# Attention heads one after the other, then a mixture of experts: the hash and the product with v start a step later in the first batch, and the sign follows its hash directly in the second

## The chip, the core and the metric

The kernel runs on one core of a Trainium2 chip. Five engines work from queues of their own, each in the order in which the program gives it work: TensorE (PE, with its weight loads as PEld), VectorE (DVE), ScalarE (ACT), GpSimd (POOL) and SyncE (SP), which issues most transfers. An engine that waits for another holds up all that stands behind the waiting instruction in its own queue. The metric is the time on the device in microseconds, as the median of several runs.

## The reference, cut to what matters

Inputs are q, k and v of shape 2 x 8 x 768 x 64 (batch, head, position, channel), a projection of 64 x 6, and the probabilities and weights of four experts.

```python
q_bits = (einsum('bhsd,dk->bhsk', q, proj) > 0)      # six hash bits per position
k_bits = (einsum('bhsd,dk->bhsk', k, proj) > 0)
mask = q_bucket[:, :, :, None] == k_bucket[:, :, None, :]
scores = where(mask, q @ k.T / sqrt(64), -1e9)
attn = softmax(scores)                                # each row
x = (attn @ v), heads side by side                    # 1536 x 512
out = sum over e of p[:, e] * (relu(x @ w1[e]) @ w2[e])
```

Everything is float32. Products that have to be exact are computed from a high and a low part of each number, as three products.

## The kernel before

**Heads and steps.** The sixteen heads (b, h) follow one another; a head has six steps, t0 to t5, one for each 128 rows of q. `attention()` is a generator that goes through the steps; in each it does the operations of `ORDER = "TXSUVMEYNRP"` in that order, and each belongs to the step by a lag:

- S (`stage_s`): four matmuls give the scores of 128 rows (two with q1 and k1, L368, and two with q2 and k2, L370, which add the mask from the hash bits). VectorE then takes the row minimum and copies the scores out of PSUM (L375). This operation is called the minimum below.
- E: ScalarE's exponential of the step before (L391).
- T, for the first nine heads (`mixed`): TensorE transposes the tile of three steps before into two PSUM tiles (L438); ScalarE and VectorE copy them out (L442, L444). In t1 and t4 ScalarE copies both, in the other steps each copies one. For the other seven heads X and Y do this with VectorE and DMA.
- V (`stage_v`): the product with v, in two parts for the first nine heads. With the lags 4 and 6 of `LAG_V` the first part stands in t3 and the second in t5 of the next head. Head (0, 7) has its own lags, 4 and 5.
- U (`stage_u`): ScalarE and VectorE copy the product out (L520, L522), in t2 of the head after that. `u_lag` adds the last lag of V and `LAG_U`: 6 + 3.
- M (`stage_m`): GpSimd divides by the row sums, for two heads at once, so only behind odd heads: the first half in t3, the second in t4 of the head two later. In the first batch each half is three GpSimd instructions (L533, L535, L538). They thus run in heads 3, 5 and 7 of the first batch.
- N: a reciprocal on VectorE (L405), in t2.
- P: the next piece of `prep_head`, the preparation of the next head.

Within one step, M and S come ahead of P.

**The preparation of a head.** `prep_head` is a generator, and each step takes one piece of it. For the heads in `BLOCKS` (2 to 8 and 11 to 15) the pieces are: in t0 VectorE transposes q and k (L293); in t1 they are split into a high part ah (ScalarE, L230) and a low part al (VectorE, L231, which needs ah), and GpSimd makes three copies of ah (L221); in t2 TensorE computes the hash, six matmuls into the PSUM tile hps (L315), and GpSimd copies al into ah; in t3 ScalarE takes the sign (L324), and GpSimd makes the bits from it (L327) and copies twelve rows (L221), after which S of the next head can run its second pair. Heads 9 and 10, (1, 1) and (1, 2), are transposed on TensorE and have one piece less: split in t0, hash in t1, sign and bits in t2. Heads 0 and 1 have code of their own.

**PSUM.** The scores, hps and the PSUM tiles of TensorE's transposes of q and k share two buffers (`big`). V, T and the expert layers share four (`one`).

**Expert weights beside the first batch.** Until the first batch is through, the main loop counts in i how often `attention()` yields; T, S and each piece of P yield once. From i = 42 on, every sixth yield gives one step of the splitting of the first weights: in most of them a cast on VectorE (L665) and a subtraction on GpSimd (L658), eight subtractions in all. A head of six steps with four pieces of P has 16 yields.

**Afterwards.** The heads of the second batch run between the matmuls of the expert layers of the first batch; then the expert layers of the second batch run alone, with fewer products.

Of the kernel before, what the change touches and what calls it, by code (L numbers as in the profile page):

```python
# [10 lines left out]
ACTF = mybir.ActivationFunctionType  # L11
# [7 lines left out]
SGN_SCALE = float(2**20)  # L19
# [4 lines left out]
LAG_T = 3  # L24
LAG_X = 2
LAG_Y = 4
LAG_V = ((4, 6), (7,))
LAST_V = (4, 5)
LAG_U = (3, 1)
LAG_M = (10, 10)  # L30
PP_BUFS = 6
TW = 3
# [17 lines left out]
def tile_lsh_attention__then__domain_moe(  # L50
# [11 lines left out]
    nc = tc.nc  # L62
    B, H, S, D = q.shape
# [12 lines left out]
    NH = S // 2  # L76
# [3 lines left out]
    MKE = MK + 2 * NB  # L80
    scale = 1.0 / float(D) ** 0.5
# [18 lines left out]
    def big(name):  # L100
        return ps2.tile([P, 2, 512], F32, tag="big", name=name)

    def one(name):
        return ps1.tile([P, 512], F32, tag="one", name=name)
# [3 lines left out]
    sgn_bias = const.tile([P, 1], F32, name="sgn_bias")  # L108
# [11 lines left out]
    def two(t):  # L120
        return t.rearrange("p (a n) -> p a n", a=2)
# [65 lines left out]
    def in_blocks(b, h):  # L187
        return b * H + h in BLOCKS
# [27 lines left out]
    def stack_tiles(b, h):  # L216
        heads[b, h] = tuple(stk.tile([P, S], F32R, tag=n, name=n) for n in ("q1", "al", "ah", "k2"))
        return heads[b, h]

    def copy_pool(dst, src):  # L220
        nc.gpsimd.tensor_scalar(out=dst, in0=src, scalar1=1.0, scalar2=1.0, op0=ALU.mult, op1=ALU.mult)  # L221
# [7 lines left out]
    def split_half(dst_hi, dst_lo, src):  # L229
        nc.scalar.activation(dst_hi, src, ACTF.Copy, scale=qk_scale)  # L230
        nc.vector.scalar_tensor_tensor(  # L231
            out=dst_lo, in0=src, scalar=qk_scale, in1=dst_hi.bitcast(F32), op0=ALU.mult, op1=ALU.subtract
        )
# [49 lines left out]
    def prep_head(b, h):  # L283
        second = (b, h) == (0, 1)
        if not second:
            tqk = loaded.pop((0, b, h))
        q1, al, ah, k2 = stack_tiles(b, h)
        if second:
            for ps, sl in zip(in_psum, halves):
                split_half(ah[:, sl], al[:, sl], ps[:, :NH])  # L290
        elif in_blocks(b, h):
            xt = ld.tile([P, S], F32, tag="tqk", name="xt")
            nc.vector.transpose(out=xt, in_=tqk.rearrange("p c r d -> p (c r d)"))  # L293
            yield 0
            split_half(two(ah), two(al), two(xt))
        else:
            ps = big("tps")
            for c in range(NT):
                nc.tensor.transpose(
                    ps[:, c // 3, (c % 3) * P : (c % 3 + 1) * P], tqk[:, c].rearrange("p a d -> p (a d)"), ident  # L300
                )
            split_half(two(ah), two(al), ps[:, :, :NH])
        for rows in (slice(0, D), slice(D, P)):
            copy_pool(q1[rows], ah[0:D].bitcast(F32))
        copy_pool(k2[0:D], ah[D:P].bitcast(F32))
        yield 654
        if second:
            yield 0
            ps = [one("hps1") for _ in range(2)]
        else:  # L310
            hps = big("hps")
            ps = [hps[:, i] for i in range(2)]
        for j, (w, a) in enumerate(((phi, ah), (plo, ah), (phi, al))):
            for i, sl in enumerate(halves):
                nc.tensor.matmul(ps[i][:MKE, :NH], w, a[:, sl], start=j == 0, stop=j == 2)  # L315
        copy_pool(ah[0:D], al[D:P].bitcast(F32))
        if second:
            for i, sl in enumerate(halves):
                nc.scalar.activation(
                    k2[D:MKE, sl], ps[i][D:MKE, :NH], ACTF.Sign, bias=sgn_bias[D:MKE], scale=SGN_SCALE  # L320
                )
        yield 978
        if not second:
            nc.scalar.activation(  # L324
                two(k2[D:MKE]), hps[D:MKE, :, :NH], ACTF.Sign, bias=sgn_bias[D:MKE], scale=SGN_SCALE
            )
        nc.gpsimd.tensor_scalar(  # L327
            out=al[D:MKE],
            in0=k2[D:MKE].bitcast(F32),
            scalar1=1.0,  # L330
            scalar2=bit_mul[D:MKE],
            op0=ALU.add,
            op1=ALU.mult,
        )
        copy_pool(k2[MQ:MQE], al[MK:MKE].bitcast(F32))
        yield 0
# [20 lines left out]
    def mixed(b, h):  # L357
        return b * H + h < LIGHT_FROM
# [189 lines left out]
    def v_lags(b, h):  # L548
        return LAST_V if (b, h) == (0, H - 1) else LAG_V[not mixed(b, h)]

    def u_lag(b, h):
        return v_lags(b, h)[-1] + (1 if (b, h) == (0, H - 1) else LAG_U[not mixed(b, h)])

# [3 lines left out]
    def attention():  # L557
# [3 lines left out]
        def do(op, i):  # L561
# [24 lines left out]
            elif op == "S":  # L586
                if i < n:
                    b, h, t = seq[i]
                    if t == 0:
                        x = hseq.index((b, h))  # L590
                        prep[0] = prep_head(*hseq[x + 1]) if x + 1 < len(hseq) else iter(())
                    stage_s(b, h, t)
                    return 652 + 4270 // NT
# [446 lines left out]
```

## Time and profile before

| | us |
|---|---|
| median of 3 runs | 745.37 (744.41 to 747.24) |
| time of the profiled execution | 746.74 |
| its span, first to last instruction | 744.8 |
| TensorE busy | 721.7 (97% of the span) |
| VectorE busy | 472.6 (63%) |
| ScalarE busy | 298.7 (40%) |
| GpSimd busy | 306.9 (41%) |

Matmuls overlap, so that TensorE's busy time is longer than the time that its array needs. The mean granted clock of TensorE was 0.995 of full speed. The first batch of heads, without expert layers beside it, ends about 146 us from the start of the span; the heads of the second batch end before 460 us.

### The profile page before, as it was taken

The numbers are of one execution on the slowest core, as the hardware profiler recorded it, in microseconds if no ns is written. First come the engines' busy times: TensorE is split into PE (matmuls) and PEld (weight loads), VectorE is DVE, ScalarE is ACT, GpSimd is POOL, SyncE is SP. The second block draws the span as 40 slices with busy tenths as digits, with TensorE's granted clock in tenths as the row PEclk, the third lists the DMA queues.
The fourth block names the chain that finished last, engine by engine and source line by source line (L and its number), as shares of the span: only waits on it lengthen the run. The fifth ranks groups of instructions, "written<-read, shape, count | busy, mean of one in ns | idle before, by whom it ended". The sixth has DMA issues, their size and how long they took to land.

```text
span 744.8 us, 10164 instructions
## 1 busy us (share of the span) xinstructions
PE 721.7 (97%) x3826; PEld 615.3 (83%) x3826; DVE 472.6 (63%) x781; ACT 298.7 (40%) x592; POOL 306.9 (41%) x279
## 2 busy tenths in 40 slices
PE   8988899999989999899999999999999999999998
PEld 6766566697987897879879888998989989899896
DVE  6677676546666666568563323798667686676763
ACT  6777677633232341332422010444334343343430
POOL 5349485423415441445142324754234342343420
PEclk9999999999999999999999999999999999999999
DMA  5224323504686797769767411243021130212302
GB/s 142 44 51 85 72 60 85 85 1 129 162 206 157 213 240 180 193 164 259 217 193 211 115 58 56 67 137 109 30 86 57 63 106 30 85 58 64 105 1 85
DMA packets 85504, 83.05 MB, mean 111 GB/s; under 512 B 49872, under 2 KB 52432, under 8 KB 85456
## 3 DMA queue, kind: packets, MB, share of 16 engines
q1 hardware_dynamic: 84432, 82.08, 40.8%
q8 instruction: 30, 0.49, 0.3%
q10 hardware_dynamic: 1024, 0.33, 0.2%
q14 instruction: 18, 0.15, 0.1%
HBM read 62.68 MB, written 19.71 MB: 111 GB/s over the span
## 4 chain that ended last, share of the span: by engine, by line
PE 87%; ACT 5%; DVE 4%; DMA 2%; issue 1%; POOL 0%; SPq 0%; DVEq 0%; POOLq 0%; ACTq 0%
PE mps L697 12%; PE mps L699 12%; PE mps L698 12%; PE pv L493 9%; PE mps L758 6%; PE mps L757 6%; PE mps L759 6%; PE sps L368 4%; PE sps L370 3%; PE ptps L438 2%; PE mps L912 2%; PE mps L908 2%; PE mps L911 2%; ACT p L391 2%; PE pd L908 2%; PE pa L912 2%
## 5 line engine op out<-in xcount | busy, mean ns | idle before, releaser
L697 PE MATMUL mps<-w2hi,hh 128*128 128x512 f32 (+1 forms) x388 | 150.7, 388 | 0.0
L699 PE MATMUL mps<-w2hi,hl 128*128 128x512 f32 (+1 forms) x388 | 150.5, 388 | 0.0
L698 PE MATMUL mps<-w2lo,hh 128*128 128x512 f32 (+1 forms) x388 | 150.4, 388 | 0.0
L375 DVE TENSOR_SCALAR_CACHE_REDUCE p<-sps 128x768 f32<-128x768 f32 x96 | 90.3, 941 | 32.9 <-PE sps L370 31.2
L391 ACT ACTIVATE p<-p,nb 128x768 f32<-128x768 f32 x96 | 89.5, 932 | 42.3 <-DVE p L375 41.8
L691 DVE SCALAR_TENSOR_TENSOR acc<-mps,pe,acc 128x512 f32<-128x512 f32 (+1 forms) x85 | 63.0, 741 | 63.0 <-PE mps L699 62.6
L763 ACT ACTIVATE hh<-mps 128x384 fp32r<-128x384 f32 x64 | 31.4, 490 | 178.5 <-PE mps L759 178.5
L758 PE MATMUL mps<-xs,w1hi 128*128 128x384 f32 x256 | 87.3, 341 | 0.6 <-POOL xs L538 0.6
L757 PE MATMUL mps<-xs,w1hi 128*128 128x384 f32 x256 | 87.7, 343 | 0.0
L759 PE MATMUL mps<-xs,w1lo 128*128 128x384 f32 x256 | 87.2, 341 | 0.0
L699 PEld LDWEIGHTS mps<-w2hi,hl 128*128 128x128 f32 x388 | 72.8, 188 | 15.6
L894 POOL TENSOR_TENSOR w2lo<-ws,w2hi 128x512 fp32r<-128x512 f32 x32 | 40.5, 1286 | 108.4 <-ACT w2hi L893 108.4
L698 PEld LDWEIGHTS mps<-w2lo,hh 128*128 128x128 f32 x388 | 72.9, 188 | 13.9
L697 PEld LDWEIGHTS mps<-w2hi,hh 128*128 128x128 f32 x388 | 72.8, 188 | 13.8
L764 DVE SCALAR_TENSOR_TENSOR hl<-mps,hh 128x384 fp32r<-128x384 f32 x64 | 35.5, 555 | 73.4 <-ACT hh L763 73.1
L658 POOL TENSOR_TENSOR w1lo<-ws,w1hi 128x512 fp32r<-128x512 f32 x32 | 42.5, 1328 | 79.6 <-DVE w1hi L665 36.1
L658 POOL TENSOR_TENSOR w2lo<-ws,w2hi 128x512 fp32r<-128x512 f32 x32 | 41.2, 1289 | 69.5 <-DVE w2hi L665 55.5
L493 PE MATMUL pv<-pt,tv 128*64 128x384 f32 x288 | 67.3, 492 | 0.0
L221 POOL TENSOR_SCALAR q<-ah 64x768 fp32r<-64x768 f32 (+1 forms) x33 | 32.4, 982 | 72.0 <-ACT ah L230 70.5
L368 PE MATMUL sps<-ah,q 128*128 128x384 f32 x192 | 54.5, 365 | 6.7 <-DVE p L375 3.7
L853 POOL TENSOR_TENSOR w1lo<-ws,w1hi 128x512 fp32r<-128x512 f32 x24 | 37.9, 1588 | 35.6 <-ACT w1hi L849 22.4
L493 PEld LDWEIGHTS pv<-pt,tv 128*64 128x64 f32 x288 | 24.8, 136 | 32.2 <-issue 31.8
(135 smaller groups left out, 1432.8 us busy)
## 6 DMA issues: line engine op xcount, KB each, us to landing
ws<-in_moe_w_dram SPq DMA_DIRECT2D x64, 512.0 KB, 4.0
scr<-t SPq DMA_DIRECT2D x14, 1152.0 KB, 8.7
pt<-scr SPq DMA_DIRECT2D x56, 288.0 KB, 6.1
tv<-in_v_dram SPq DMA_DIRECT2D x16, 192.0 KB, 4.5
out_dram<-acc SPq DMA_DIRECT2D x11, 256.0 KB, 2.0
rdb<-row SPq DMA_DIRECT2D x14, 192.0 KB, 5.2
tqk<-in_q_dram SPq DMA_DIRECT2D x26, 96.0 KB, 3.3
tqk<-in_k_dram SPq DMA_DIRECT2D x24, 96.0 KB, 3.4
```

Of the source, the lines that this page charges most:

```text
L368: nc.tensor.matmul(ps[:, i, :NH], q1[:, sl], k1[:, i * NH : (i + 1) * NH], start=True, stop=False)
L375: nc.vector.tensor_scalar(out=two(pt), in0=ps[:, :, :NH], scalar1=MASKED, scalar2=MASKED, op0=ALU.min, op1=ALU.min, accum_out=nb,)
L391: nc.scalar.activation(pt, pt, ACTF.Exp, bias=nb, scale=-1.0, accum_out=dens[b, h, r][:, o : o + 1])
L493: nc.tensor.matmul(dst, vvs[b, h][:, c], pts[b, h, g][c], start=c == 0, stop=c == NT - 1, tile_position=(0, g * D),)
L658: nc.gpsimd.tensor_tensor(out=lo[:, c - 1], in0=st[c - 1], in1=hi[:, c - 1].bitcast(F32), op=ALU.subtract)
L691: nc.vector.scalar_tensor_tensor(out=acc, in0=ps, scalar=pcol, in1=acc, op0=ALU.mult, op1=ALU.add)
L697: nc.tensor.matmul(ps, hh[:, ts], w2hi[:, f, cs], start=n == 0, stop=False)
L698: nc.tensor.matmul(ps, hh[:, ts], w2lo[:, f, cs], start=False, stop=False)
L699: nc.tensor.matmul(ps, hl[:, ts], w2hi[:, f, cs], start=False, stop=n == FC - 1)
L757: nc.tensor.matmul(ps[:, :SB], w1hi[:, kk, fs], xhi[b, kk][:, sl], start=kk == 0, stop=False)
L758: nc.tensor.matmul(ps[:, :SB], w1hi[:, kk, fs], xlo[b, kk][:, sl], start=False, stop=False)
L759: nc.tensor.matmul(ps[:, :SB], w1lo[:, kk, fs], xhi[b, kk][:, sl], start=False, stop=kk == KD - 1)
```

## The change

Three things change. For heads 2 to 8 (prepared in heads 1 to 7 of the first batch) one empty piece stands ahead of the hash, so that the hash moves from t2 to t3 and the sign with the bits from t3 to t4. For the first nine heads the product with v moves by a step: the first part from t3 to t4, the second from t5 of the next head to t0 of the head after; U stays in t2. For heads 9 to 15 the sign is given right behind the hash, ahead of the next step; the bits stay in t3, and move from t2 to t3 for heads 9 and 10. Heads 2 to 8 have five pieces now, so the head in which they are prepared has 17 yields.

```diff
-LAG_V = ((4, 6), (7,))
+LAG_V = ((5, 7), (7,))
-LAG_U = (3, 1)
+LAG_U = (2, 1)
...
         copy_pool(k2[0:D], ah[D:P].bitcast(F32))
         yield 654
+
+        def sign():
+            nc.scalar.activation(
+                two(k2[D:MKE]), hps[D:MKE, :, :NH], ACTF.Sign, bias=sgn_bias[D:MKE], scale=SGN_SCALE
+            )
+
+        if mixed(b, h) and (second or in_blocks(b, h)):
+            yield 0
         if second:
-            yield 0
             ps = [one("hps1") for _ in range(2)]
         else:
             hps = big("hps")
...
+        if not mixed(b, h):
+            sign()
         yield 978
-        if not second:
-            nc.scalar.activation(
-                two(k2[D:MKE]), hps[D:MKE, :, :NH], ACTF.Sign, bias=sgn_bias[D:MKE], scale=SGN_SCALE
-            )
+        if b and h and not in_blocks(b, h):
+            yield 0
+        if mixed(b, h) and not second:
+            sign()
         nc.gpsimd.tensor_scalar(
             out=al[D:MKE],
```

## Rows read from the trace of the kernel before

**Rows 1.** Windows: length, busy us (count) of PE, PEld, DVE, ACT, POOL; granted clock, DMA.

```profile
22.00:146.00 124.00, 113.00 (x707) 80.00 (x707) 84.14 (x166) 89.85 (x187) 72.40 (x76) 1.00 0.35 72
146.00:460.00 314.00, 308.53 (x1591) 264.48 (x1590) 175.82 (x307) 87.26 (x176) 114.54 (x102) 0.99 0.61 163
```

**Rows 2.** Waits of TensorE from 20 to 140 us: total, times, longest.

```profile
PE hps L315 <- DVE al L231: 4.7, 6, 0.8
PE hps L315 <- ACT ah L230: 4.7, 7, 1.1
```

**Rows 3.** Timeline, TensorE in head 4: start, us, instruction, count, idle time before.

```profile
65.69 0.87 PE L438 MATMUL ptps<-ident,p 128*128 128x128 f32 x6
...
70.56 0.60 PE L315 MATMUL hps<-ah,phi 128*108 128x384 f32 x2 [0.59 <-ACT ah L230]
71.00 0.51 PE L315 MATMUL hps<-ah,plo 128*108 128x384 f32 x2
72.28 0.61 PE L315 MATMUL hps<-al,phi 128*108 128x384 f32 x2 [0.77 <-DVE al L231]
```

**Rows 4.** Chain of waits, the pieces that follow: start, us, work.

```profile
73.62 0.62 PE sps L368 x2
74.24 0.36 PE sps L370 x2
74.60 2.09 PE pv L493 x12
```

**Rows 5.** Timeline, VectorE in the same stretch.

```profile
70.61 1.62 DVE L231 SCALAR_TENSOR_TENSOR al<-xt,qk_scale,ah 128x768 fp32r<-128x768 f32 x1 [0.60 <-ACT ah L230]
...
72.62 0.94 DVE L375 TENSOR_SCALAR_CACHE_REDUCE p<-sps 128x768 f32<-128x768 f32 x1
...
73.60 0.56 DVE L520 COPY xf<-pv 64x384 f32<-64x384 f32 x1
...
74.76 0.95 DVE L375 TENSOR_SCALAR_CACHE_REDUCE p<-sps 128x768 f32<-128x768 f32 x1
```

**Rows 6.** Timeline, ScalarE in the same stretch.

```profile
66.28 0.49 ACT L444 ACTIVATE pth<-ptps 128x384 f32<-128x384 f32 x1 [1.73 <-PE ptps L438]
...
67.92 0.85 ACT L444 ACTIVATE pth<-ptps 128x384 f32<-128x384 f32 x2
68.66 0.94 ACT L391 ACTIVATE p<-p,nb 128x768 f32<-128x768 f32 x1
...
69.58 0.93 ACT L230 ACTIVATE ah<-xt,qk_scale 128x768 fp32r<-128x768 f32 x1
```

**Rows 7.** Timeline, GpSimd in head 3, a head with M.

```profile
54.72 2.33 POOL L221 TENSOR_SCALAR q<-ah 64x768 fp32r<-64x768 f32 x2 [6.45 <-ACT ah L230]
...
57.92 0.83 POOL L221 TENSOR_SCALAR ah<-al 64x768 fp32r<-64x768 f32 x1
...
60.13 1.20 POOL L533 TENSOR_TENSOR xf<-xf,rdb 128x384 f32<-128x384 f32 x1
...
63.12 0.91 POOL L327 TENSOR_SCALAR al<-k,bit_mul 44x768 fp32r<-44x768 f32 x1
...
65.07 1.19 POOL L533 TENSOR_TENSOR xf<-xf,rdb 128x384 f32<-128x384 f32 x1
...
67.91 2.53 POOL L658 TENSOR_TENSOR w1lo<-ws,w1hi 128x512 fp32r<-128x512 f32 x2
```

**Rows 8.** Timeline, TensorE: the two long idle times in the second batch.

```profile
208.96 0.61 PE L368 MATMUL sps<-ah,q 128*128 128x384 f32 x2 [2.41 <-ACT k L324]
...
307.65 0.61 PE L368 MATMUL sps<-ah,q 128*128 128x384 f32 x2 [2.34 <-DVE p L375]
```

**Rows 9.** Windows behind the first of them, columns as in rows 1.

```profile
210.00:212.00 2.00, 2.00 (x8) 2.00 (x7) 0.92 (x2) 0.00 (x0) 0.83 (x1) 0.50 1.02 224
212.00:214.00 2.00, 2.00 (x9) 2.00 (x9) 0.00 (x0) 0.39 (x1) 0.00 (x0) 0.65 1.06 220
```

**Rows 10.** Timeline, VectorE in head 7: the same split as in rows 5.

```profile
118.61 1.02 DVE L231 SCALAR_TENSOR_TENSOR al<-xt,qk_scale,ah 128x768 fp32r<-128x768 f32 x1 [0.52 <-ACT ah L230]
```

## The prediction

> **What bounds the kernel now.** I read the windows by stage first. From 146 to 460 us TensorE is busy for 308.5 of 314 us at a clock of 0.99; in the first batch, 22 to 146 us, for 113.0 of 124 us, although no other engine is busy for more than 90 [rows 1]. So the first batch has idle time to win, and the rest has it only in single gaps. The waits of TensorE name the gaps of the first batch: 4.7 us for ah and 4.7 us for al, all ahead of the hash [rows 2]. The timelines of one head show what surrounds them [rows 3 to 6], that of GpSimd what the bits compete with [rows 7]. The second batch has two gaps of 2.4 us [rows 8].
>
> **One head before.** I count from the T that follows the second part of V, at 65.69 us [rows 3]. TensorE stood ready for the hash at 70.56 - 0.59 = 69.97: three steps of T and S in 4.28, 1.43 each. It waits for ah, runs the pairs 0.44 apart, waits 0.77 for al, and has the last pair at 6.59 [rows 3]. S of t3 starts at 7.93 and V at 8.91 [rows 4]. S starts 0.02 behind the minimum of t2, which ran from 6.93 until U began at 7.91 [rows 5]: the scores take turns in two PSUM buffers, and the hash held the other. So VectorE's queue, al, copy, minimum, releases S, and the waits for ah and al lie inside that chain.
>
> **The first batch, chain of splits.** The order of heavy work on TensorE stays as it was (hash, V, a light step, V, two light steps); all of it moves one step against the split. I count again from the T behind the second part of V, which is now that of t1. ScalarE can begin its copies 0.59 behind T's start (66.28 against 65.69), takes 0.85 for the two, 0.92 for the exponential (68.66 to 69.58) [rows 6], and al begins 1.03 behind the start of ah's split (69.58 to 70.61) [rows 5, 6]: 3.39, where it was 4.92. That is the gain, 1.53 us.
>
> It is given back. S of t2 and S of t3 now hold both buffers when the hash comes, so the hash must take that of t2 and wait for its minimum. In VectorE's queue this stands behind al. From al to that minimum's start it is 2.01, to its end 2.99 (70.61, 72.62, 73.60) [rows 5]: the hash starts at 6.4, with TensorE ready at 4.3. S of t4 needs the buffer of t3, and that minimum starts 4.15 behind al (74.76) [rows 5] and takes 0.98: 8.52. The array would be ready sooner: three pairs at 0.44 and less than 0.62 for T end by 8.4. S thus starts at 8.55, V 0.98 later at 9.53 [rows 4], against 8.91: **+0.62 us a head**, seven heads, **+4.3 us**. Which buffer the hash takes hardly matters, since S of t4 needs the minimum of t3 either way.
>
> The bounds: al took 1.62 in five of the seven heads and 1.02 in two [rows 5, 10]. With 1.02 in all, the chain is 0.6 shorter in those five (+1.3 in all); with 1.62 in all it is 0.6 longer in two (+5.5). I take the mixture of now.
>
> The Trainium skill has a rule for this ("SBUF — State Buffer", section "SBUF: two separate sides"): VectorE with two SBUF inputs and GpSimd share a port pair, and whichever starts first holds it for the whole instruction. Both begin here when ah is there; the two durations in rows 5 and 10 agree with such a race. By the rule the change could also turn it, and if VectorE won in all heads, the sum below would be 3 us less; that is one of the rivals.
>
> **The first batch, bits on GpSimd.** The bits stood ahead of M's second half; now they come behind it, since M precedes P and both are in t4. What waits for them is the second pair of S in the next head's t0, which now stands ahead of V, two steps behind the first part: 9.53 + 2.09 [rows 4] + 2 x 1.43 - 0.36 = 14.1. In heads without M the bits are in time: the sign follows an exponential of 0.94 [rows 6] that the minimum at 8.52 releases, and the two bit instructions take 1.95 (63.12 to 65.07) [rows 7]; even with a sign as long again as the exponential all of it ends near 12.4.
>
> In head 3 GpSimd starts at 3.4 with ah and then runs in order: three copies 3.2 (54.72 to 57.92), a subtraction of weights 1.3 (half of 2.53), M's first half 3.0 (60.13 to 63.12), the copy of al 0.9, another subtraction 1.3, M's second half 2.8 (65.07 to 67.91), bits 1.95 [rows 7]. That ends at 17.8, **3.7 us late**. Where the subtractions fall I get from the count of yields: with 17 a head, head 3 begins at i = 48, so that i = 54 (t2) and i = 60 (t4) bring one each; head 5 begins at 82 and gets one in t2 (i = 90), that of i = 96 comes behind the bits; head 7 gets none. So head 5 ends 1.3 earlier (2.4 late) and head 7 2.6 earlier (1.1 late): **+7.2 us**. Below, the bound is nothing, if GpSimd keeps up; above, 3.7 in each, +11.1.
>
> **The clock behind long waits.** After both idle times of 2.4 us in the second batch [rows 8] the granted clock was 0.50 and then 0.65 for 2 us each [rows 9], that is, 1.2 instead of 2.4 GHz for most of it: (0.50 + 0.35) x 2 = 1.7 us lost. After the 1.1 us in front of the hash the stage stayed at 1.00 [rows 1, 2]. Waits of 3.7 and 2.4 us are like the former, that of 1.1 like the latter: 2 x 1.7 = **+3.4 us**, between 0 and 5.1.
>
> **The second batch.** At 208.96 S waited 2.41 for the sign, which sat on ScalarE behind an exponential that came late [rows 8]. With the sign behind the hash the buffer is free long before: -2.41 - 1.7 = **-4.1 us**, at least -2.4. The other gap, 2.34, is for a minimum on VectorE [rows 8], in the buffer that S takes next whatever the sign does; I leave it at 0, with -4.1 as the other end. ScalarE's waiting for the hash costs nothing: the expert layers that its next instructions serve stand behind the hash on TensorE too, and it is busy for 87 of 314 us [rows 1]. V of (1, 0) a step later falls among expert layers, and the later bits of heads 9 and 10 have three steps left: nothing, as long as TensorE has such work to do. No transfer moves past another on SyncE's queue.
>
> **Sum.** 4.3 + 7.2 + 3.4 - 4.1 = +10.8 us. Profiled, 746.74 + 10.8 = 757.5; the median shown lies 1.4 lower, so 745.37 + 10.8 = **756.2 us**.
>
> **The rivals.**
> - *The waits go and nothing takes their place* (faster). -9.4 [rows 2] - 4.1 = 731.9. It decides if VectorE ends the minimum of t3 by the time TensorE reaches S of t4 without waiting, near 6.2, and GpSimd is in time. For it: no engine but TensorE is over 73% busy in this stage [rows 1]. Against it: in order, the chain comes to 8.5. With part of the gain it ends between 732 and 741. Chance 0.16.
> - *Only one of the two queues is late.* With the chain but bits in time, 745.4 + 4.3 - 4.1 = 745.6. With no chain, GpSimd late: four heads without M win the waits (four sevenths of 9.4 = 5.4), three lose 7.2 and 3.4, less 4.1: 746.5. For the first: GpSimd has idle time of 51.6 of 124 us [rows 1]; against it, none of it lies where the three heads need it [rows 7]. Chance 0.20.
> - *Both gaps of the second batch go*, if S takes the buffer that the sign freed: 756.2 - 4.1 = 752.1. Chance 0.10.
> - *VectorE wins the port in all heads*: 756.2 - 3.0 = 753.2. Chance 0.06.
> - The forecast, 750 to 761 by its bounds: 0.48.
>
> **Range and chances.** About 0.5%, 3.7 us, is what a measurement of this kernel can tell from no change. The first rival holds what is faster (0.16), the second what is the same (0.20), the rest is slower (0.64). The range goes from 742, with the first rival below it, to 761; beyond that I leave 0.04.
>
> **What would show it.** Right: the hash waits for a minimum (L375) and no longer for ah and al; the second pair of S (L370) waits for GpSimd's copy k in heads 4, 6 and 8, longest in head 4, with the clock at half behind it; GpSimd has L327 behind L538 of M's second half; the wait of 2.41 us for L324 is gone, and the one for L375 near 307 us remains. Wrong: the windows of the first batch get shorter than 124 us for the same work, or L370 has no wait there. What would upset it most is a GpSimd order in which M's second half does not stand ahead of the bits.

## The result and the profile after

The changed kernel takes 755.91 us (median of 4 runs, 754.36 to 758.54) against 745.04 for the kernel before (4 runs): a ratio of 1.0144, 95% interval 1.0104 to 1.0184. It is 1.4% slower; 756.2 had been forecast. The profiled execution took 757.32 us with a span of 755.6, 10.8 us more than the span before.

Where the time went is seen best at the matmuls of the first layer of the experts. They run beside the second batch of heads and begin when the first batch is done. By line, of the kernel before: count, durations, first and last start.

```profile
L757 PE MATMUL mps<-xs,w1hi x256: 333/334/522, 145.6 to 476.1; 128*128 128x384 f32 x128
```

The same line of the changed kernel, where it has the number 766:

```profile
L766 PE MATMUL mps<-xs,w1hi x256: 333/334/444, 164.4 to 486.4; 128*128 128x384 f32 x128
```

The first batch ends 164.4 - 145.6 = 18.8 us later. From the first of these matmuls to the last it takes 322.0 instead of 330.5 us: 8.5 are won back. What follows is as long as before within 0.5 us (269.2 and 268.7). So the change holds a loss and a gain, and both are larger than forecast (14.9 and 4.1).

**Waits of TensorE in the first batch** (20 to 170 us, after; total, times, longest), in place of [rows 2]:

```profile
PE hps L322 <- DVE p L384: 9.1, 6, 1.9
PE sps L379 <- POOL k L221: 5.1, 3, 2.3
PE sps L377 <- DVE p L384: 2.9, 5, 1.4
...
PE hps L322 <- DVE rd L414: 1.7, 1, 1.7
```

The 9.4 us of waiting for ah and al are gone but for 0.8, and the hash waits 9.1 us for the minimum instead. In head 1 it waits 1.7 us for the instruction behind that minimum in VectorE's queue (the last line). The second line is new: the second pair of S waits three times for GpSimd. Smaller waits of T for ScalarE, 2.2 us in all, are new too.

**The chain in head 7.** Timeline of the changed kernel, TensorE (start, us, instruction, count, idle time before); compare [rows 3, 4]:

```profile
131.66 0.87 PE L447 MATMUL ptps<-ident,p 128*128 128x128 f32 x6
...
137.96 0.61 PE L322 MATMUL hps<-ah,phi 128*108 128x384 f32 x2 [1.43 <-DVE p L384]
...
140.22 0.62 PE L377 MATMUL sps<-ah,q 128*128 128x384 f32 x2 [0.31 <-DVE p L384]
...
141.13 0.54 PE L502 MATMUL pv<-pt,tv 128*64 128x384 f32 x1
...
147.03 0.62 PE L379 MATMUL sps<-k,al 76*128 76x384 f32 x2 [1.23 <-POOL k L221]
```

and VectorE, to compare with [rows 5]:

```profile
134.96 1.61 DVE L231 SCALAR_TENSOR_TENSOR al<-xt,qk_scale,ah 128x768 fp32r<-128x768 f32 x1 [0.71 <-ACT ah L230]
...
136.96 0.94 DVE L384 TENSOR_SCALAR_CACHE_REDUCE p<-sps 128x768 f32<-128x768 f32 x1
...
137.94 0.56 DVE L529 COPY xf<-pv 64x384 f32<-64x384 f32 x1
...
139.21 0.95 DVE L384 TENSOR_SCALAR_CACHE_REDUCE p<-sps 128x768 f32<-128x768 f32 x1
```

Read the two together. The hash starts 0.02 behind the start of U, that is, when the minimum of t2 has ended, and S of t4 when that of t3 has. Both minima stand behind al in VectorE's queue, and al waits for ah.

**The bits in head 3.** Timeline of GpSimd after, to compare with [rows 7], and the matmuls of TensorE that wait for it:

```profile
57.77 2.32 POOL L221 TENSOR_SCALAR q<-ah 64x768 fp32r<-64x768 f32 x2 [5.93 <-PE ptps L447]
...
61.13 1.28 POOL L667 TENSOR_TENSOR w1lo<-ws,w1hi 128x512 fp32r<-128x512 f32 x1
62.37 1.21 POOL L542 TENSOR_TENSOR xf<-xf,rdb 128x384 f32<-128x384 f32 x1
...
66.32 1.27 POOL L667 TENSOR_TENSOR w1lo<-ws,w1hi 128x512 fp32r<-128x512 f32 x1
67.55 1.20 POOL L542 TENSOR_TENSOR xf<-xf,rdb 128x384 f32<-128x384 f32 x1
...
70.54 0.91 POOL L336 TENSOR_SCALAR al<-k,bit_mul 44x768 fp32r<-44x768 f32 x1
71.53 0.83 POOL L221 TENSOR_SCALAR k<-al 12x768 fp32r<-12x768 f32 x1
...
72.41 1.01 PE L379 MATMUL sps<-k,al 76*128 76x384 f32 x2 [2.27 <-POOL k L221]
```

GpSimd is hardly idle here (13.8 of 14.6 us busy, no gap above 0.12 us): both halves of M and two subtractions of weights run ahead of the bits (L336), and S goes on 0.05 us behind the last of them.

**The clock.** Windows after (length, busy times as in [rows 1], then the granted clock) in the stretches where it fell:

```profile
62.00:64.00 2.00, 2.00 (x9) 1.85 (x9) 1.84 (x5) 0.42 (x3) 1.91 (x3) 0.50 0.04 2
64.00:66.00 2.00, 2.00 (x11) 1.56 (x11) 0.42 (x1) 1.82 (x5) 1.83 (x3) 0.71 0.00 0
72.00:74.00 2.00, 1.59 (x4) 0.80 (x6) 0.55 (x1) 0.00 (x0) 1.62 (x2) 0.50 0.67 251
74.00:76.00 2.00, 2.00 (x10) 0.75 (x8) 1.31 (x3) 0.00 (x0) 0.00 (x0) 0.50 0.00 0
76.00:78.00 2.00, 2.00 (x9) 0.82 (x6) 0.00 (x0) 0.00 (x0) 0.00 (x0) 0.50 0.51 81
```

The fall at 62 us follows the longest wait of the hash for the minimum, 1.93 us in head 3; that at 72 us the wait of 2.27 us for GpSimd, and it costs twice as much (3.4 us) as the one in [rows 9]. A third, from 112 to 118 us, follows the wait of 1.56 us for GpSimd in head 5, and the earliest, from 27 to 32 us, the hash's wait of 1.74 us in head 1. In this profiled execution the first batch lost 8.5 us to the clock ((1 - clock) x length, added over windows of 10 us), where it had lost nothing in that of the kernel before. That is not one us of time for each us of clock: two executions of the changed kernel took 754.36 and 754.50 us at mean clocks of 0.986 and 0.993, 5 us of clock apart.

**The second batch.** Timeline after, at the place where the gap of 2.34 us had been [rows 8]:

```profile
317.81 0.90 ACT L309 ACTIVATE k<-hps,sgn_bias 44x768 fp32r<-44x768 f32 x1
...
319.32 0.51 PE L377 MATMUL sps<-ah,q 128*128 128x384 f32 x2
...
319.57 0.43 DVE L674 CAST w2hi<-ws 128x512 fp32r<-128x512 f32 x1 [3.56 <-DMA ws<-in_moe_w_dram]
...
320.81 0.92 DVE L384 TENSOR_SCALAR_CACHE_REDUCE p<-sps 128x768 f32<-128x768 f32 x1
```

VectorE still waits for the weights, 3.56 us, and the minimum is as late as it was. But S starts 1.49 us before that minimum, which reads the scores of the step before: S must have taken the other buffer, the one that the sign freed at 318.71. No wait of TensorE for VectorE or ScalarE is left from 158 us to the end.

### The profile page after: what moved, and what is told of

Its sections match the earlier page's. It is cut to its first block, busy times and chain, and to the rows that moved or that the text cites. A ratio compares the mean times of both kernels' runs of the same rounds, so it can differ in the third digit from the quotient of the medians.

```text
span 755.6 us, 10170 instructions
## 1 busy us (share of the span) xinstructions
PE 725.9 (96%) x3826; PEld 619.1 (82%) x3826; DVE 473.1 (63%) x781; ACT 300.6 (40%) x592; POOL 305.8 (40%) x279
## 4 chain that ended last, share of the span: by engine, by line
PE 87%; POOL 4%; DVE 4%; ACT 3%; issue 1%; DMA 0%; ACTq 0%; POOLq 0%; DVEq 0%
PE mps L706 12%; PE mps L708 12%; PE mps L707 12%; PE pv L502 9%; PE mps L766 6%; PE mps L767 6%; PE mps L768 6%; PE sps L379 3%; PE sps L377 3%; PE ptps L447 3%; PE mps L921 2%; PE mps L917 2%; PE mps L920 2%; PE pd L917 1%; PE pa L921 1%; PE pd L921 1%
## 5 line engine op out<-in xcount | busy, mean ns | idle before, releaser
L767 PE MATMUL mps<-xs,w1hi 128*128 128x384 f32 x256 | 86.0, 336 | 0.6 <-POOL xs L547 0.6
L766 PE MATMUL mps<-xs,w1hi 128*128 128x384 f32 x256 | 86.4, 338 | 0.0
L706 PEld LDWEIGHTS mps<-w2hi,hh 128*128 128x128 f32 x388 | 72.9, 188 | 13.8
L667 POOL TENSOR_TENSOR w1lo<-ws,w1hi 128x512 fp32r<-128x512 f32 x32 | 42.4, 1326 | 88.7 <-DVE w1hi L674 59.1
L502 PE MATMUL pv<-pt,tv 128*64 128x384 f32 x288 | 70.9, 504 | 0.0
L379 PE MATMUL sps<-k,al 76*128 76x384 f32 x192 | 50.9, 346 | 5.5 <-POOL k L221 5.1
```

The costliest lines, as they stand in the source:

```text
L379: nc.tensor.matmul(ps[:, i, :NH], q2[0:MQE, sl], k2[0:MQE, i * NH : (i + 1) * NH], start=False, stop=True)
L502: nc.tensor.matmul(dst, vvs[b, h][:, c], pts[b, h, g][c], start=c == 0, stop=c == NT - 1, tile_position=(0, g * D),)
L667: nc.gpsimd.tensor_tensor(out=lo[:, c - 1], in0=st[c - 1], in1=hi[:, c - 1].bitcast(F32), op=ALU.subtract)
L706: nc.tensor.matmul(ps, hh[:, ts], w2hi[:, f, cs], start=n == 0, stop=False)
L766: nc.tensor.matmul(ps[:, :SB], w1hi[:, kk, fs], xhi[b, kk][:, sl], start=kk == 0, stop=False)
L767: nc.tensor.matmul(ps[:, :SB], w1hi[:, kk, fs], xlo[b, kk][:, sl], start=False, stop=False)
```

## The experiments

Each time stands against the kernel before, run beside it on the same chip: 746.47 us for the first four, 746.03 for the next four, 746.93 for the last two. The changed kernel was not run beside them. Differences from its 755.91 us are differences of times; the kernel before had 745.04 us beside it, so by the ratios the gains on it come out up to 2 us larger. "L" numbers are those of each kernel.

**1. The sign of the second batch alone.**

```diff
+        if not mixed(b, h):
+            sign()
         yield 978
-        if not second:
...
+        if mixed(b, h) and not second:
+            sign()
```

> Of the change only the sign behind the hash in the second batch (heads 9 to 15); the first batch as before. Theory: S takes the PSUM buffer that the earlier sign has freed, so both idle times of TensorE in the second batch (2.41 and 2.34 us, each with 1.7 us of clock behind it) go, whatever the first batch does: 745.0 - 8.2 = 736.8 us, first batch of the old length. Rival: only the gap that waited for the sign goes, and the other went in the changed kernel because the first batch had shifted the weight transfers: 745.0 - 4.1 = 740.9, with a wait for the minimum of some 2.3 us left near 303 us.

Measured: 739.26 us, ratio 0.9904 (0.9878 to 0.9930), 7.2 us faster. From the first to the last expert matmul (L763 here, L757 before) it takes 321.8 us (330.5 before), and TensorE waits for no other engine from 150 us on. Both gaps go with the sign alone; the first batch has nothing to do with it.

**2. The first batch alone.**

```diff
-        if not mixed(b, h):
-            sign()
         yield 978
-        if b and h and not in_blocks(b, h):
-            yield 0
-        if mixed(b, h) and not second:
+        if not second:
             sign()
```

(against the changed kernel)

> Of the change only the first batch (hash and product with v a step later); sign of the second batch as before. Theory: the first batch is 18.8 us longer, both gaps of the second batch are there again: 745.0 + 18.8 = 763.8 us. Rival (the second gap depends on how the first batch shifts the rest): one gap alone, 759.7.

Measured: 764.3 us, ratio 1.0243 (1.0224 to 1.0262), 17.8 us slower. Experiments 1 and 2 add up: 17.8 - 7.2 = 10.6, and the change cost 10.9. The two gaps are back, from 165 us on (waits of TensorE: total, times, longest):

```profile
PE sps L373 <- DVE p L380: 2.6, 1, 2.6
PE sps L373 <- ACT k L309: 2.4, 1, 2.4
```

**3. One half of M less ahead of the bits.**

```diff
-LAG_M = (10, 10)
+LAG_M = (11, 10)
```

(against the changed kernel)

> The changed kernel with the division by the row sums a step later in the first batch, so that one half of it instead of two stands ahead of the bits on GpSimd. Theory: GpSimd is 2.8 us earlier with the bits in heads 3, 5 and 7; the waits of S's second pair for GpSimd (2.3, 1.7 and 1.1 us, 5.1 in all) fall to under 0.5 us in all, and with them the half clock behind two of them (5.1 us lost): 755.9 - 10 = 746 us. Rival: the waits only cover what VectorE's chain would cost anyway, and S waits as long for another engine: 751 us or more.

Measured: 748.14 us, ratio 1.0019 (1.0003 to 1.0034): 7.8 us less than the changed kernel. No wait of S for GpSimd is left. In the profiled execution the clock is no better: it lost 8.5 us in the first batch here too, behind waits of the hash for VectorE, of 1.43 to 2.41 us. That execution was the slowest of ten, at the lowest mean clock, 0.989; the others had 0.990 to 0.998, against 0.986 to 0.993 for the changed kernel. So the waits for GpSimd are shown as a cause, worth about their own length and some more; the falls of the clock do not hang on them alone.

**4. The hash later, V at its old place.**

```diff
-LAG_V = ((5, 7), (7,))
+LAG_V = ((4, 6), (7,))
-LAG_U = (2, 1)
+LAG_U = (3, 1)
```

(against the changed kernel)

> The changed kernel with the product with v at its old place: hash, sign and bits of heads 2 to 8 a step later alone, and the sign of the second batch. Theory: the first part of V now stands between S of t3 and the hash and covers al, the copy and the minimum on VectorE, so the hash hardly waits (some 0.1 us instead of 1.4) and a head without late bits takes about 14.5 us instead of 15.9; the bits are late in the heads with M, by 3.8, 2.5 and 1.2 us with 3 to 5 us of clock: -10 + 7.5 + 4 - 8.2, about 738 us. Rival: a hash in t3 costs wherever V stands: 752 us or more.

Measured: 742.4 us, ratio 0.9953 (0.9936 to 0.9970). With the 7.2 us of experiment 1 taken off, the first batch is some 3 us longer than before. The hash waits no more, as expected, but the heads without late bits (no wait of S for GpSimd) take 15.83 us from V to V, as before (15.87), and not 14.5. The waits of TensorE from 20 to 150 us say where it went:

```profile
PE sps L379 <- POOL k L221: 3.4, 2, 2.5
PE sps L377 <- DVE p L384: 3.0, 8, 0.4
...
PE pv L502 <- DVE pth L451: 2.8, 5, 0.6
```

V now stands in the hash's old place, and needs the copy of the transposes that VectorE makes behind al. In the timeline al runs from 88.25 (1.61 us), the copy begins at 89.79, and V at 90.39:

```profile
89.79 0.55 DVE L451 COPY pth<-ptps 128x384 f32<-128x384 f32 x1
...
90.39 0.54 PE L502 MATMUL pv<-pt,tv 128*64 128x384 f32 x1 [0.56 <-DVE pth L451]
```

My theory of the gain was wrong: what stands third behind V waits for the same chain, whether it is the hash or V.

**5. al behind the minimum.**

```diff
             yield 0
-            split_half(two(ah), two(al), two(xt))
+            split_hi(two(ah), two(xt))
...
+        if mixed(b, h) and in_blocks(b, h):
+            split_lo(two(al), two(xt), two(ah))
         if mixed(b, h) and (second or in_blocks(b, h)):
             yield 0
```

(against the changed kernel)

> The changed kernel with VectorE's part of the split (al) moved into the empty piece of t2, behind the copy and the minimum of that step and behind U; ScalarE's part stays in t1. Theory: the hash's 9.1 us of waiting for the minimum go, since that minimum no longer stands behind al; al then comes some 5 to 6 us behind T of t1, the hash waits for it by about 1, and S of t4 starts near 7.8 instead of 8.5. Seven heads by 0.7, one fall of the clock (1.7) less, late bits 2 us more: 755.9 - 5 = 751 us. Rival: VectorE's total work in the light steps is the bound, not its order: 755 to 757.

Measured: 753.47 us, ratio 1.0091 (1.0058 to 1.0124), 2.4 us less than the changed kernel, with ratios that overlap; it had been expected to be 5 less. The waits from 20 to 165 us:

```profile
PE sps L390 <- POOL k L221: 10.3, 3, 5.0
PE hps L333 <- DVE al L233: 5.0, 8, 0.8
```

The hash's wait for the minimum is gone, and the four intervals from V to V without late bits are 15.2 to 16.2 us long (16.5 to 18.0 in the changed kernel), so the order in VectorE's queue was the cause of that wait. Some of the difference is al itself, which took 0.97 to 1.31 us here instead of 1.6. But the time is spent again at GpSimd: TensorE reaches S earlier, the bits are no earlier, and the three waits double from 5.1 to 10.3.

**6. V later alone.**

```diff
-LAG_V = ((4, 6), (7,))
+LAG_V = ((5, 7), (7,))
-LAG_U = (3, 1)
+LAG_U = (2, 1)
```

(against the kernel before)

> The kernel before with the product with v a step later alone; hash, sign and bits as before. Theory: with two light steps instead of three between V and the hash S of t3 still waits for the minimum behind al, a head takes as long as before, and the bits, in t3 behind one half of M, are just in time: 746 us within 2. Rival: V a step later costs by itself, since the hash comes a step nearer to the end of V: 750 us or more.

Measured: 749.92 us, ratio 1.0056 (1.0035 to 1.0077), 3.9 us slower, at the edge of the rival. The waits from 20 to 150 us:

```profile
PE hps L315 <- DVE al L231: 4.7, 6, 0.8
PE hps L315 <- ACT ah L230: 3.0, 7, 1.1
PE sps L368 <- ACT k L324: 2.5, 6, 0.7
```

The hash waits as before, but nothing stands between the hash and two steps of S any more, and S of t4 waits for the sign that frees hps: 2.5 us in six heads. A head takes 16.23 us instead of 15.87. I had left the sign out.

**7. The preparation ahead of the exponential, with the sign of experiment 1.**

```diff
-ORDER = "TXSUVMEYNRP"
+ORDER = "TXSUVMPEYNR"
```

> The kernel with the sign of the second batch alone, and the preparation put ahead of the exponential in each step (P before E), so that ah stands ahead of an exponential on ScalarE. Theory: al is what the chain waits for; VectorE would be free for it 0.55 us earlier than ah comes now, so a head gets shorter by about 0.5: 739.3 - 3.9 = 735.4 us. Rival: the later exponentials hold up T: 739 us or more.

Measured: 735.23 us, ratio 0.9863 (0.9844 to 0.9882), 10.8 us faster than the kernel before and the lowest time of all, though its ratio overlaps with those of experiments 1 and 8. The waits of the hash from 20 to 145 us:

```profile
PE hps L315 <- DVE al L231: 3.0, 5, 0.8
PE hps L315 <- ACT ah L230: 1.7, 5, 0.8
PE hps L315 <- DVE p L381: 1.5, 2, 0.9
```

The first two were 4.7 and 4.7 [rows 2]; the third is new. ah leaves ScalarE ahead of an exponential, and al, which everything else in VectorE's queue stands behind, follows it.

**8. Experiment 4 with M a step later.** `LAG_M = (11, 10)` in that kernel.

> Hash a step later with V at its old place and the sign of the second batch, and the division by the row sums a step later. Theory: the waits of S's second pair for GpSimd (3.4 us) and the one fall of the clock behind them (1.7 us) go: 742.4 - 5 = 737.4 us, heads of 15.85 us throughout. Rival: 741 us or more, with the same time lost to VectorE.

Measured: 736.63 us, ratio 0.9879 (0.9863 to 0.9896). The wait for GpSimd falls from 3.4 to 0.3 us, and the time by 5.8 against experiment 4.

**9. Experiment 8 with the preparation ahead of the exponential.** The `ORDER` of experiment 7 in the kernel of experiment 8.

> Hash a step later with V at its old place, sign of the second batch, division a step later, and the preparation ahead of the exponential. Theory: V of t3 waits for the copy behind al, as the hash does elsewhere; ah comes some 0.5 us earlier and so does that copy: 736.6 - 3.5 = 733 us. Rival: at this length of a head ScalarE and VectorE are full and the order no longer matters: 735 us or more.

Measured: 739.01 us, ratio 0.9892 (0.9877 to 0.9906), 2.4 us more than experiment 8 by its own time, though the two ratios overlap. The gain did not come: T now waits for the exponential that ah has overtaken, and behind the longest of these waits (1.69 us) the clock fell in the profiled execution, by 1.7 us. From 20 to 150 us:

```profile
PE ptps L447 <- ACT p L400: 9.6, 8, 1.7
```

**10. The preparation ahead of M and the exponential in the changed kernel.**

```diff
-ORDER = "TXSUVMEYNRP"
+ORDER = "TXSUVPMEYNR"
```

> The changed kernel with the preparation ahead of the division and the exponential in each step (P before M), so that the bits no longer stand behind M's second half. Theory: the waits of S's second pair for GpSimd (5.1 us) and the fall of the clock behind them (5.1 us) go, and ah comes earlier by the length of an exponential, which the chain of al gets back in seven heads (5 us at most): 755.9 - 10.2 - 5 = 741 us. Rival: 746 us or more, if the chain does not follow ah; 752 or more, if the bits are not the cause.

Measured: 739.77 us, ratio 0.9904 (0.9888 to 0.9921), 16.1 us less than the changed kernel. The waits for GpSimd fall from 5.1 to 0.7 us, the clock stays up in the profiled run (mean 1.0), and the hash's wait for the minimum falls from 9.1 to 4.2; in its place T waits 3.8 us for the exponential. So another order within a step takes back most of the loss of the first batch. The step itself still costs something: experiment 7, with the preparation ahead of the exponential too but hash and V at their old places, is 4.5 us faster (3.1 by the ratios).

## Why the prediction came out right, and where it did not

**The time** was forecast as 756.2 and measured as 755.9, but two terms were off by about 4 us each in opposite directions: the first batch lost 18.8 instead of 14.9, the second won 8.5 instead of 4.1. That the total came out within 0.3 us is luck.

**The chain of splits** (+0.62 a head) held step by step. In head 7, counted from T at 131.66: al was forecast at 3.39 and came at 3.30, the hash at 6.4 and came at 6.30, S of t4 at 8.55 and came at 8.56, V at 9.53 and came at 9.47. From V of head 6 to V of head 7 it takes 16.50 us, 0.63 more than a head before. The hash waits for the minimum of t2, S for that of t3, as forecast; experiment 5 shows that the order in VectorE's queue is what makes the first of them late. Head 3 lost more than 0.62: a weight cast ahead of the minimum made the hash's wait 1.93 us, and the clock fell behind it. I had left the casts out of the sum; no experiment takes them away.

**The bits on GpSimd** (+7.2) came out as 5.1. The queue was sized well: from the first copy to the end of the bits 14.4 us were forecast for head 3, and it took 72.36 - 57.77 = 14.6. The waits were forecast as 3.7, 2.4 and 1.1, and measured as 2.27, 1.56 and 1.23: in heads 3 and 5 V had been held up itself, by a cast ahead of a minimum in both and by the clock in head 3, so S asked later. Experiment 3 takes these waits away and leaves the hash's 9.1 us; experiment 10 takes away more than half of both.

**The clock** (+3.4) was undersized: 8.5 us in the first batch. The waits that I judged by were those above 2.3 us; here it also fell behind waits of 1.93 and 1.56 us, not behind those of 1.43 and 1.23 in head 7, and once it cost twice as much. So of the 18.8 us 5.1 are waits for GpSimd (7.2 forecast), 8.5 the clock (3.4), and the rest, 5.2, stands against 4.3 for the chain. This rest is by subtraction, in one execution, and holds the casts too; how much of the lost clock lies beside waits that would have been there anyway is not shown. That a wait of such a length brings the clock down was itself no safe step: in experiment 2 it stayed up behind the same wait of 2.27 us, and in experiment 3 it fell behind two of 1.43 us.

**The second batch** (-4.1): the step that failed is that the second gap is "for a minimum on VectorE, in the buffer that S takes next whatever the sign does". The trace after shows S ahead of that minimum, so in the other buffer, and experiment 1 shows that the sign alone brings this about. That was one of the rivals; it had 0.10.

**The rivals.** The first, that nothing takes the waits' place, fell on the chain, as it should. Of *only one of the two queues is late* experiments 3 and 10 are the nearest: with GpSimd in time the first batch still loses, until ah is moved as well. In the race of al with GpSimd's copy VectorE lost in six of seven heads (1.61 us; 1.02 in one), so it did not win in all. GpSimd's copy starts 0.01 to 0.02 us ahead of al in the six, and 0.04 behind it in the one. This agrees with the Trainium skill ("SBUF — State Buffer", section "SBUF: two separate sides"), by which the first to start holds the shared port pair for the whole instruction. In the kernel before one head does not fit: in head 5 al is recorded 0.04 us ahead of the copy (86.41 against 86.45) and took 1.68 us.

**What stays open**: what decides whether the clock falls behind a wait and how long it stays down. In experiment 1 it fell at 26 us, behind waits of the hash of 1.12 and 0.77 us; in experiment 10 it stayed up behind one of 1.52 us.

## What to carry to other kernels

When a waiting instruction moves away from its wait, look for what else is behind the late work in the same queue: here the hash, V, and S all stood behind one split on VectorE. An earlier ah helped in experiments 7 and 10; in experiment 9 it did not, since T then waited for what ah had overtaken. A step later is not a step more of slack if the work that stands ahead of it in its engine's queue, within that step, grows: the bits lost theirs to M. An early release of one of two PSUM buffers can be worth more than the wait it ends, because the next user is no longer tied to the other; the sign alone gave 7.2 us.

## What the runs showed of the hardware

TensorE's granted clock fell from 2.4 to 1.2 GHz behind waits of 1.56 us (head 5), 1.74 us (head 1), 1.93 and 2.27 us (head 3) in the changed kernel, and not behind its waits of 1.43 us. After the wait of 2.27 us it stayed at 0.50 in all three windows from 72 to 78 us, while the fall behind the first gap of the kernel before was over after some 4 us [rows 9]. The length of a single wait does not decide it. In experiment 2 the clock stayed at 1.00 behind the same wait in head 3, and the pair behind it took 0.62 us, where it took 1.01 in the changed kernel:

```profile
73.08 0.62 PE L375 MATMUL sps<-k,al 76*128 76x384 f32 x2 [2.27 <-POOL k L221]
```

In experiment 3 it fell behind a wait of the hash of 1.43 us in head 4 (0.94 us for a pair that takes 0.60 at full clock):

```profile
80.24 0.94 PE L322 MATMUL hps<-ah,phi 128*108 128x384 f32 x2 [1.43 <-DVE p L384]
```
